# A decode step of attention and a gated MLP: four heads per load of keys or values, 17 loads for 28, with a new order on DVE and PE

## The chip, the cores and the metric

The kernel runs on one core of a Trainium2 chip. The metric is the device time of one execution in microseconds (us), the median of several runs. Engines: PE (matrix multiply), DVE (vector), ACT (scalar functions), POOL (general purpose) and SP, whose queue here does nothing but issue DMAs.

## The reference, cut to what matters

One token x (1 x 576, bf16) is normalized, then goes through attention over the last 4096 positions of a cache with 16 key/value heads, each shared by two query heads (32 query heads of width 128), and through a gated MLP. Both results are added to x.

```
W = 4096                                    # of 65536 positions
q = (xn @ wq).reshape(1, 1, 32, 128)        # wq: 576 x 4096
k = repeat(k_cache[:, :, -W:, :], 2)        # 16 heads x 4096 x 128
v = repeat(v_cache[:, :, -W:, :], 2)
p = softmax(q . k * 128 ** -0.5)
o = (p . v).reshape(4096) @ wo              # wo: 4096 x 576
z = gelu(xn @ w_in)                         # w_in: 576 x 4608
z1, z2 = z[:2304], layernorm(z[2304:])
out = x + o + (z1 * (w_sp * z2 + b_sp)) @ w_out   # w_out: 2304 x 576
```

Keys and values are 16.8 MB each, all inputs that are read 51 MB. Every byte is used once.

## The kernel before, in words

The order of the work is written by hand: each engine runs its instructions in the order in which the program issues them (`manual_schedule`), and waits where a tile is not ready or its buffer is not free.

**Loads.** All large loads are issued by SP, one queue, in program order (L99 to L111): wq in three pieces, the keys of heads 0 to 3, w_in in three pieces, then keys and values in turn, two heads (2.1 MB) per load, then w_out and wo in five pieces. They go into a ring of 7 buffers of 20,736 bytes per partition. A load waits until the readers of the load seven places earlier are done, and every later load on SP waits behind it. In a load of keys, partition r x 2 + h holds 64 consecutive positions of head h (16 KB).

**Start.** xn is laid out in a column, split into XT; 36 matmuls give q (L225, `qps`), which is copied (L232), spread over partitions (L240, `qps2`) and written as `Qb` (L249): for each head four small stationary operands (`be`), one for each part of the transposed layout below. 

**Keys.** Heads are handled in groups of four, g = 0 to 3. `t_half(m, hf)` (L262) turns half of a load of two heads with two DVE transposes of 128 x 1024 fp32 words (each word a pair of bf16), in blocks of 32 x 32. `s_half(m, hf)` (L271) then makes the scores on PE: per head four matmuls (`be`) of 512 columns that accumulate in the PSUM tile `S[g % 2]`, each head at its own 32 columns of the PE (`tile_position`).

**Softmax.** `sm_a(g)` (L296) takes the row maximum on DVE, spreads it over the partitions of a head by two small transposes (`spread`, L284; the whole chain takes 2.3 us, 97.91 to 100.20), and lets ACT write exp of the scores into `pz[g % 2]`, two instructions for a group (L305), with the row sums in `lx`. `sm_b(g)` (L309) transposes `pz` on DVE into `pt` (called tr(g) below) and copies `pt` on ACT into `PT` with 16 small copies (L321), so that positions stand on partitions.

**Values.** `sums(g)` (L324) adds up the row sums with a matmul; `recip(g)` (L331) inverts them. `pv(g)` (L338) is 32 matmuls of 512 columns into the PSUM tile `ops`, at four column positions in turn. `norm(g)` (L351) takes the wanted diagonal of `ops` on DVE, `y_mms(g)` (L361) arranges it on PE, `y_copy(g)` (L371) writes the bf16 column `Y`. The small PSUM tiles (`lps`, `yps`, `psz`) share one buffer, so each waits for the reader of the one before it.

**MLP.** `z_mms` (L375) is 162 small matmuls with w_in as the stationary operand; `z_exp`, `z_gelu` and `z_norm` (L385 to L427) are short DVE, ACT, POOL and PE steps that give `hv`.

**Order.** The loop at L429 runs over 16 halves: transposes of the half, its scores, and between them the softmax of the group before and the values of the group before that. The MLP's DVE work stands in group 1. After the loop (L474): norm and y_mms of group 2, `sm_b(3)`, `pv(3)`, two thirds of `out_hv` (w_out, 36 matmuls in all, L470) while DVE does `norm(3)`, then `y_mms(3)`, the last third, and 64 matmuls of wo (L488), all into `acc`. Two copies and a DMA end the kernel.

Of the kernel before, what the change touches and what calls it, by code (L numbers as in the profile page):

```python
# [22 lines left out]
NT = W // 128  # L23
GK = 4
NG = HKV // GK
NP = HKV // 2
TP = 2 * NT
# [6 lines left out]
RING = 7  # L34
NS = 9
SLOT = NF * D
# [3 lines left out]
def kernel(  # L40
# [19 lines left out]
    ring = ctx.enter_context(tc.tile_pool(name="ring", bufs=RING))  # L60
    const = ctx.enter_context(tc.tile_pool(name="const", bufs=1))
    work = ctx.enter_context(tc.tile_pool(name="work", bufs=2))
    ktpool = ctx.enter_context(tc.tile_pool(name="ktpool", bufs=3))
# [11 lines left out]
    def ring_tile(name, rows, width):  # L75
        t = ring.tile([P, SLOT], BF16, name=name, tag="ring")
        return t[:, 0:rows * width].rearrange("p (s c) -> p s c", c=width)

    def load_halves(src, lo, n, name):

        v = ring_tile(f"{name}{lo}", n, src.shape[1] // 2)
        rows = src.rearrange("r (e c) -> (r e) c", e=2).rearrange("(p s) c -> p s c", s=NS)
        nc.sync.dma_start(v, rows[:, lo:lo + n, :])  # L83
        return [(lo + s, v[:, s, :]) for s in range(n)]

    def load_kv(src, m, name):

        t = ring.tile([P, SLOT], BF16, name=f"{name}{m}", tag="ring")
        v = t[:, 0:TP * DH]
        nc.sync.dma_start(v, src[0, 2 * m:2 * m + 2, SK - W:SK, :].rearrange("h (r t) d -> r h (t d)", t=TP))  # L90
        return v.rearrange("p (t d) -> p t d", d=DH)

    def load_n(src, per, lo, n, name):
        v = ring_tile(f"{name}{lo}", n, D)
        nc.sync.dma_start(v, src.rearrange("(p t) n -> p t n", t=per)[:, lo:lo + n, :])
        return [(lo + t, v[:, t, :]) for t in range(n)]

    K, V = {}, {}
    wq_sb = load_halves(A_wq, 0, 2, "wq") + load_halves(A_wq, 2, 4, "wq") + load_halves(A_wq, 6, 3, "wq")  # L99
    for m in range(2):  # L100
        K[m] = load_kv(A_k_cache, m, "k")
    win_sb = sum((load_halves(B_w_in, lo, 3, "win") for lo in (0, 3, 6)), [])
    for m in range(2, NP):
        K[m] = load_kv(A_k_cache, m, "k")
        V[m - 2] = load_kv(A_v_cache, m - 2, "v")
    for m in range(NP - 2, NP):
        V[m] = load_kv(A_v_cache, m, "v")
    wout_sb = load_n(B_w_out, NF, 0, NF, "wout")
    wo_sb = []
    for n in (14, 9, 6, 2, 1):  # L110
        wo_sb += load_n(A_wo, 32, len(wo_sb), n, "wo")  # L111
# [28 lines left out]
    idv = ident[:].rearrange("p (q c hh) -> p q c hh", q=4, hh=4)[:, :, 0:4, :]  # L140
    cm = const.tile([P, 4], FP32, name="cm")
    nc.vector.tensor_reduce(out=cm[:], in_=idv.rearrange("p q c hh -> p c q hh"), op=ALU.add,
                            axis=mybir.AxisListType.XY)
    dmask = const.tile([P, 4, DH], FP32, name="dmask")
    nc.gpsimd.tensor_copy(dmask[:], cm[:].unsqueeze(2).to_broadcast([P, 4, DH]))
    ohm = const.tile([P, 2, 4], FP32, name="ohm")
    for pr in range(2):
        nc.vector.tensor_reduce(out=ohm[:, pr, :], in_=idv[:, 2 * pr:2 * pr + 2].rearrange("p q c hh -> p hh q c"),
                                op=ALU.add, axis=mybir.AxisListType.XY)
# [3 lines left out]
    selv = sel[:].rearrange("p q (r hh e) -> p q r hh e", r=2, hh=4)  # L153
    for dq in range(4):
        nc.gpsimd.tensor_copy(selv[:, dq, :, :, dq], ohm[:])

    ids = ident[:].rearrange("p (i a h) -> p i a h", i=4, h=2)[:, :, 0:4, :]
    oha = const.tile([P, 4, 2], FP32, name="oha")
    nc.vector.reduce_sum(oha[:], ids.rearrange("p i a h -> p i h a"), axis=AXX)

    lsum = const.tile([P, 4, 8, 2, 2], FP32, name="lsum")
    nc.gpsimd.memset(lsum[:], 0.0)
    for hd in range(2):
        for pr in range(2):
            for th in range(2):
                nc.gpsimd.tensor_copy(lsum[:, 2 * pr + th, 0:4, hd, :],
                                      oha[:, 2 * hd + pr, :].unsqueeze(1).to_broadcast([P, 4, 2]))

    pz = []
    for n in range(2):  # L170
        t = const.tile([P, TP, 16, 2], BF16, name=f"pz{n}")
        nc.gpsimd.memset(t[:], 0.0)
        pz.append(t)
# [88 lines left out]
    def t_half(m, hf):  # L262

        kT = ktpool.tile([P, NT, 2, 16, 2, 2], BF16, name=f"kT{m}_{hf}", tag="kT")
        src = K[m][:, NT * hf:NT * (hf + 1), :].rearrange("p t d -> p (t d)").bitcast(FP32)
        dst = kT[:].rearrange("p t b r x e -> p (t b r x e)").bitcast(FP32)
        for n in range(2):
            nc.vector.transpose(dst[:, 1024 * n:1024 * (n + 1)], src[:, 1024 * n:1024 * (n + 1)])  # L268
        KT[m, hf] = kT

    def s_half(m, hf):  # L271
        g, pr = divmod(m, 2)
        kv = KT.pop((m, hf))[:].rearrange("p t b r x e -> p b e x t r")
        for hd in range(2):
            i = 2 * hd + pr
            for be in range(4):
                nc.tensor.matmul(  # L277
                    S[g % 2][32 * i:32 * i + 8, hf, :],
                    lhsT=Qb[:, 2 * m + hd, be].rearrange("p a h -> p (a h)"),
                    rhs=kv[:, be // 2, be % 2, hd],  # L280
                    start=(be == 0), stop=(be == 3), tile_position=(0, 32 * i),
                )
# [13 lines left out]
    def sm_a(g):  # L296
        s = S[g % 2]
        nc.vector.tensor_reduce(out=mx[:, 0:1], in_=s[:], op=ALU.max, axis=mybir.AxisListType.XY)  # L298
        bk = spread(mx, mb, g, ALU.max, "m")
        nm = work.tile([P, 1], FP32, name=f"nm{g}", tag="nm")  # L300
        nc.vector.tensor_scalar_mul(nm[:], bk[:, 0:1], -SCALE)  # L301
        p = pz[g % 2]
        for hd in range(2):
            lo, hi = 64 * hd, 64 * hd + 64
            nc.scalar.activation(p[lo:hi, :, :, hd], s[lo:hi].rearrange("p a (t r) -> p (a t) r", r=16), ACT.Exp,  # L305
                                 bias=nm[lo:hi, 0:1], scale=SCALE, accum_out=lx[lo:hi, g:g + 1])
        st[g] = {"p": p}

    def sm_b(g):  # L309
        d = st[g]  # L310
        pt = work.tile([P, TP, 32], BF16, name=f"pt{g}", tag="pt")
        src = d["p"][:].rearrange("p t r x -> p (t r x)")
        dst = pt[:].rearrange("p t x -> p (t x)")
        for n in range(2):
            nc.vector.transpose(dst[:, 1024 * n:1024 * (n + 1)], src[:, 1024 * n:1024 * (n + 1)])  # L315
        PT = work.tile([P, 2, TP, 2, 2], BF16, name=f"PT{g}", tag="PT")
        pt4 = pt[:].rearrange("p t x -> p (t x)").bitcast(FP32).rearrange("p (t x) -> p t x", x=16)
        PT4 = PT[:].rearrange("p r t x h -> p (r t x h)").bitcast(FP32).rearrange("p (r t x) -> p r x t", r=2, x=2)
        for i in range(GK):
            for a in range(4):  # L320
                nc.scalar.copy(PT4[32 * a:32 * a + 32, i % 2, i // 2, :], pt4[32 * i:32 * i + 32, :, a])  # L321
        d["PT"] = PT

    def sums(g):  # L324

        lps = ps_m.tile([P, 32], FP32, name=f"lps{g}", tag="m")
        nc.tensor.matmul(lps[:, 0:1], lhsT=lsum[:].rearrange("p q c x h -> p (q c x h)"), rhs=lx[:, g:g + 1],  # L327
# [10 lines left out]
    def pv(g):  # L338

        d = st[g]  # L340
        for tb in range(NT // 4):
            for q in range(4):
                pr, t0 = q // 2, NT * (q % 2) + 4 * tb
                nc.tensor.matmul(  # L344
                    ops[32 * q:32 * q + 16, :],
                    lhsT=d["PT"][:, pr, t0:t0 + 4].rearrange("p t x h -> p (t x h)"),
                    rhs=V[2 * g + pr][:, t0:t0 + 4, :],
                    start=(tb == 0), stop=(tb == NT // 4 - 1), tile_position=(0, 32 * q),
# [79 lines left out]

    for j in range(2 * NP):  # L429
        g, o = divmod(j, GK)  # L430
        t_half(j // 2, j % 2)
        if o == 3:
            if g > 0:
                recip(g - 1)
            if g > 1:
                norm(g - 2)
        s_half(j // 2, j % 2)
        if g > 0 and o == 1:
            if g > 1:
                sm_b(g - 1)  # L440
            else:
                G, sz = z_gelu(*z_exp(zps))

                acc = []
                for n, pool in enumerate((ps_a, ps_b)):
                    t = pool.tile([P, 512], FP32, name=f"acc{n}", tag="ab"[n])
                    acc.append(t[32 * n:32 * n + 1, 0:CW])
                    nc.tensor.matmul(acc[n], lhsT=ones_b[:, 0:1], rhs=xrow[:, CW * n:CW * (n + 1)],
                                     start=True, stop=False, tile_position=(0, 32 * n))
                hv = z_norm(G, sz)  # L450
        if g > 0 and o == 2:
            sums(g - 1)
        if o == 3:
            if g > 1:
                y_mms(g - 2)
            sm_a(g)
            if g > 1:
# [67 lines left out]
```

## Time and profile before

| | us |
|---|---|
| median of 3 runs | 127.36 (127.31 to 127.39) |
| span of the profiled execution | 125.4 |
| between that span and the median of the runs | 1.9 |
| PE, DVE, ACT busy | 68.4, 78.5, 33.6 |
| 32 transposes of keys (L268) | 36.9 |
| 128 score matmuls (L277), union of their records | 32.3 |
| 128 value matmuls (L344), the same | 11.7 |
| 64 copies of PT (L321) | 18.9 |
| 8 exp (L305) | 11.2 |

The span runs from the first to the last instruction of one execution; an execution's own time beside its span is not recorded, so the 1.9 us are taken from the runs. In the rows of the profile, "out<-in" names the tiles written and read, "L" the line above, and what stands behind "<-" in brackets is what ended the idle time before the instruction. The page cuts the span into 40 slices of 3.1 us and gives a digit for the busy share of each, in tenths; DMA is the share of the core's 16 DMA engines, PEclk the clock that PE was granted.

### The profile page before, as it was taken

The page shows a single profiled execution, that of the slowest core. Times are in us where ns is not written, and L with a number is a line of the kernel's source. Part 1 is how long each engine was busy: PE and PEld are TensorE (multiplying, and loading weights), DVE is VectorE, ACT ScalarE, POOL GpSimd, SP SyncE. Part 2 cuts the span into 40 slices and gives each one's busy share as a digit, 9 for nine tenths or more (in the row PEclk, how much of TensorE's full clock was granted, in tenths as well). Part 3 has the DMA queues.
Part 4 walks back from the last instruction along what each step waited for, and adds up shares of the span by engine and source line. Part 5 has one row for each costly group of instructions (what it writes and reads, how often), then busy time and mean ns, then how long its engine had stood idle before and what let it go on. Part 6 is the DMA issues. An engine that isn't in the chain of part 4 may idle for free.

```text
span 125.4 us, 1630 instructions
## 1 busy us (share of the span) xinstructions
PE 68.4 (55%) x626; PEld 31.4 (25%) x626; DVE 78.5 (63%) x150; ACT 33.6 (27%) x85; POOL 7.9 (6%) x27
## 2 busy tenths in 40 slices
PE   0034810398999668069257049639029811178862
PEld 0021110112699612014011012411003511024640
DVE  6853049997517595794798298899098967005001
ACT  4000030000072950000441940260860092920001
POOL 2991000000000000100000000000000000000000
PEclk9999995558975555959958977986955996557998
DMA  4999999999999999999999999999999999999960
GB/s 115 455 423 422 425 434 439 422 428 435 428 438 418 434 434 428 423 444 423 428 439 434 413 439 434 428 428 434 428 436 434 428 426 439 434 409 427 416 261 0
DMA packets 4047, 51.06 MB, mean 407 GB/s; under 512 B 454, under 2 KB 584, under 8 KB 840
## 3 DMA queue, kind: packets, MB, share of 16 engines
q1 hardware_dynamic: 4032, 50.96, 95.6%
q8 instruction: 5, 0.08, 0.2%
q14 instruction: 2, 0.02, 0.0%
q10 hardware_dynamic: 8, 0.00, 0.0%
HBM read 50.96 MB, written 0.00 MB: 406 GB/s over the span
## 4 chain that ended last, share of the span: by engine, by line
DMA 71%; PE 11%; DVE 11%; issue 2%; SPq 1%; ACT 1%
DMA k<-in_A_k_cache_dram 44%; DMA wo<-in_A_wo_dram 17%; DMA wq<-in_A_wq_dram 10%; DVE kT L268 6%; PE S L277 5%; PE ops L344 3%; DVE Qb L255 2%; PE qps L227 1%; PE acc L467 1%; DVE q_rep L238 1%; ACT q_rep L236 1%; DVE on L358 1%; PE lps L327 1%; SPq L83 1%; DVE om L354 1%
## 5 line engine op out<-in xcount | busy, mean ns | idle before, releaser
L277 PE MATMUL S<-kT,Qb 128*8 128x512 bf16 x128 | 32.3, 636 | 30.3 <-DVE kT L268 30.3
L268 DVE STREAM_TRANSPOSE kT<-k 128x1024 f32<-128x1024 f32 x32 | 36.9, 1212 | 8.3 <-DMA k<-in_A_k_cache_dram 8.3
L305 ACT ACTIVATE pz<-S,nm 64x1024 bf16<-64x1024 f32 x8 | 11.2, 1406 | 45.0 <-DVE nm L301 30.3
L321 ACT COPY PT<-pt 32x64 f32<-32x64 f32 x64 | 18.9, 295 | 14.6 <-DVE pt L315 13.8
L277 PEld LDWEIGHTS <-Qb 128*8 128x8 bf16 x128 | 6.4, 96 | 49.7 <-issue 46.7
L344 PE MATMUL ops<-v,PT 128*16 128x512 bf16 x128 | 11.7, 441 | 3.5 <-ACT PT L321 3.5
L315 DVE STREAM_TRANSPOSE pt<-pz 128x1024 bf16<-128x1024 bf16 x8 | 9.4, 1212 | 4.1 <-ACT pz L305 4.1
L380 PEld LDWEIGHTS <-win 128*128 128x128 bf16 x162 | 10.1, 165 | 0.9 <-issue 0.9
L380 PE MATMUL zps<-XT,win 128*128 128x2 bf16 x162 | 10.2, 201 | 0.0
L354 DVE SCALAR_TENSOR_TENSOR om<-ops,rs,dmask 128x512 f32<-128x512 f32 x4 | 3.0, 742 | 7.4 <-PE ops L344 7.3
L298 DVE TENSOR_REDUCE mx<-S 128x1 f32<-128x1024 f32 x4 | 4.9, 1220 | 3.7 <-PE S L277 3.7
L344 PEld LDWEIGHTS <-PT 128*16 128x16 bf16 x128 | 5.0, 97 | 7.3 <-ACT PT L321 4.1
L227 PE MATMUL qps<-wq,XT 128*2 128x512 bf16 x36 | 4.2, 621 | 2.3 <-DVE XT L218 1.9
L467 PE MATMUL acc<-wo,Y 128*1 128x288 bf16 x64 | 4.6, 285 | 1.3 <-DMA wo<-in_A_wo_dram 1.3
L236 ACT CAST q_rep<-qps 128x512 bf16<-128x512 f32 x2 | 1.2, 585 | 14.0 <-DVE q_rep L238 14.0
L238 DVE CAST q_rep<-qps 128x512 bf16<-128x512 f32 x2 | 1.4, 692 | 5.1 <-PE qps L227 4.5
L193 PE MATMUL ps_x<-ones_b,xtw 1*128 1x1 bf16 x9 | 0.4, 162 | 7.2 <-DVE xtw L191 7.2
L492 DVE CAST res<-acc 1x288 bf16<-1x288 f32 x1 | 0.4, 446 | 6.1 <-PE acc L467 6.1
L358 DVE TENSOR_REDUCE on<-om 128x128 f32<-128x512 f32 x4 | 4.1, 1034 | 0.1
L327 PE MATMUL lps<-lx,lsum 128*128 128x1 f32 x8 | 2.1, 333 | 3.2 <-DVE Y L372 3.2
L493 ACT CAST res<-acc 1x288 bf16<-1x288 f32 x1 | 0.4, 389 | 12.4 <-PE acc L467 12.4
L467 PEld LDWEIGHTS <-Y 128*1 128x1 bf16 x64 | 2.9, 83 | 3.0 <-issue 1.9
(90 smaller groups left out, 46.8 us busy)
## 6 DMA issues: line engine op xcount, KB each, us to landing
k<-in_A_k_cache_dram SPq DMA_DIRECT2D x8, 2048.0 KB, 27.2
v<-in_A_v_cache_dram SPq DMA_DIRECT2D x8, 2048.0 KB, 27.8
win<-in_B_w_in_dram SPq DMA_DIRECT2D x3, 1728.0 KB, 27.1
wout<-in_B_w_out_dram SPq DMA_DIRECT2D x1, 2592.0 KB, 30.2
wq<-in_A_wq_dram SPq DMA_DIRECT2D x1, 2048.0 KB, 9.3
wo<-in_A_wo_dram SPq DMA_DIRECT2D x1, 2016.0 KB
wq<-in_A_wq_dram SPq DMA_DIRECT2D x1, 1536.0 KB, 12.5
wo<-in_A_wo_dram SPq DMA_DIRECT2D x1, 1296.0 KB
```

Source lines behind the costliest of these rows:

```text
L227: nc.tensor.matmul(qps[32 * g:32 * g + 2, :], lhsT=XT[:, s, :], rhs=wv[:, 512 * g:512 * (g + 1)], start=(s == 0), stop=(s == NS - 1), tile ...
L268: nc.vector.transpose(dst[:, 1024 * n:1024 * (n + 1)], src[:, 1024 * n:1024 * (n + 1)])
L277: nc.tensor.matmul(S[g % 2][32 * i:32 * i + 8, hf, :], lhsT=Qb[:, 2 * m + hd, be].rearrange("p a h -> p (a h)"), rhs=kv[:, be // 2, be % 2 ...
L298: nc.vector.tensor_reduce(out=mx[:, 0:1], in_=s[:], op=ALU.max, axis=mybir.AxisListType.XY)
L305: nc.scalar.activation(p[lo:hi, :, :, hd], s[lo:hi].rearrange("p a (t r) -> p (a t) r", r=16), ACT.Exp, bias=nm[lo:hi, 0:1], scale=SCALE, ...
L315: nc.vector.transpose(dst[:, 1024 * n:1024 * (n + 1)], src[:, 1024 * n:1024 * (n + 1)])
L321: nc.scalar.copy(PT4[32 * a:32 * a + 32, i % 2, i // 2, :], pt4[32 * i:32 * i + 32, :, a])
L344: nc.tensor.matmul(ops[32 * q:32 * q + 16, :], lhsT=d["PT"][:, pr, t0:t0 + 4].rearrange("p t x h -> p (t x h)"), rhs=V[2 * g + pr][:, t0:t ...
L354: nc.vector.scalar_tensor_tensor(out=om[:].rearrange("p c d -> p (c d)"), in0=ops[:], scalar=d["rs"][:, 0:1], in1=dmask[:].rearrange("p c ...
L358: nc.vector.reduce_sum(on[:], om[:].rearrange("p c d -> p d c"), axis=AXX)
L380: nc.tensor.matmul(zps[:, :, t], lhsT=wt[:, t, :], rhs=XT[:, s, :], start=(s == 0 and t == 0), stop=(s == NS - 1 and t == NF - 1), skip_gr ...
L467: nc.tensor.matmul(acc[n], lhsT=lhs[:, col:col + 1], rhs=wv[:, CW * n:CW * (n + 1)], start=False, stop=last, tile_position=(0, 32 * n))
```

## The change

- **Loads.** A load of keys or values has four heads, a whole group (4.2 MB, 32 KB per partition; partition r x 4 + h, 128 positions each). There are four slots of 32 KB per partition, a to d, one small one (f), and a fixed place for each load: wq (8 rows) in a, wq's ninth row and the last two rows of w_in in parts of d, K0 in b, K1 in c, then w_in a, K2 b, V0 c, K3 d, V1 a, V2 b, V3 c, w_out a, wo in pieces of 18 (d), 10 (b), 3 (c) and 1 (f). All keys are ahead of V1. 17 loads stand where 28 stood. They are still issued by SP in this order.
- **Keys and scores.** `keys(g, c)` turns half of a load of four heads with four transposes of the same size; `scores(g, c)` makes 16 matmuls of 512 columns, with the heads in the inner loop, so that the column position changes with each matmul. The columns are now (pair of position blocks, r, s): neighbouring columns are 128 elements apart. The transposed keys have two buffers of twice the size, not three.
- **Softmax.** exp takes four instructions of 32 partitions for a group. `pz` is one tile for all groups, not two; `pt` is one fp32 tile; the transposes of `sm_b` move fp32 words (two of 1024, as before in number), and its 16 copies have 2 x 64 columns, not 64.
- **Values.** The stationary operand of `pv` has 32 columns, not 16, and all four positions read one load.
- **Constants.** `cm`, `dmask`, `ohm`, `sel`, `oha` and `lsum` follow the new layout with as many or fewer small instructions.
- **Order.** A written list takes the place of the loop. `tail(g)` is recip, norm, y_mms and y_copy. pv(1), tail(1), pv(2) and tail(2) stand after the last scores and ahead of sm_b(3); all of `out_hv` stands behind tail(3).

The diff, cut to its core (what it takes out of the loads and of the loop is in the listing above):

```diff
 W = 4096
 F = 4608
 FH = 2304
...
 GK = 4
 NG = HKV // GK
...
+TP = W // 32
+TC = TP // 2
 NR = 98
 NF = FH // 128
 CW = D // 2
 EPS = 1e-5
 SCALE = DH ** -0.5
 GELU_C = 0.7978845608028654
-RING = 7
 NS = 9
...
     lead = ctx.enter_context(tc.tile_pool(name="lead", bufs=1))
-    ring = ctx.enter_context(tc.tile_pool(name="ring", bufs=RING))
+    big = ctx.enter_context(tc.tile_pool(name="big", bufs=1))
     const = ctx.enter_context(tc.tile_pool(name="const", bufs=1))
     work = ctx.enter_context(tc.tile_pool(name="work", bufs=2))
-    ktpool = ctx.enter_context(tc.tile_pool(name="ktpool", bufs=3))
+    ktpool = ctx.enter_context(tc.tile_pool(name="ktpool", bufs=2))
+    single = ctx.enter_context(tc.tile_pool(name="single", bufs=1))
...
+    def rows(slot, src, name, lo, n, at=None):
+        w = src.shape[1]
+        if at is None:
+            t = big.tile([P, n * w], BF16, name=f"{name}{lo}", tag=slot)[:]
+        else:
+            t = slot[:, at:at + n * w]
+        v = t.rearrange("p (s c) -> p s c", c=w)
+        nc.sync.dma_start(v, src.rearrange("(p s) c -> p s c", p=P)[:, lo:lo + n, :])
         return [(lo + s, v[:, s, :]) for s in range(n)]
...
+    def load_kv(slot, src, g, name):
+        t = big.tile([P, TP * DH], BF16, name=f"{name}{g}", tag=slot)
+        nc.sync.dma_start(t[:], src[0, GK * g:GK * g + GK, SK - W:SK, :].rearrange("h (r t) d -> r h (t d)", t=TP))
+        return t[:].rearrange("p (t d) -> p t d", d=DH)
+    wq_h = A_wq.rearrange("r (e c) -> (r e) c", e=2)
+    win_h = B_w_in.rearrange("r (e c) -> (r e) c", e=2)
     K, V = {}, {}
...
+    rest = big.tile([P, TP * DH], BF16, name="rest", tag="d")
+    wq_sb = rows("a", wq_h, "wq", 0, 8) + rows(rest, wq_h, "wq", 8, 1, 0)
+    K[0] = load_kv("b", A_k_cache, 0, "k")
+    K[1] = load_kv("c", A_k_cache, 1, "k")
+    win_sb = rows("a", win_h, "win", 0, 7) + rows(rest, win_h, "win", 7, 2, 2048)
+    K[2] = load_kv("b", A_k_cache, 2, "k")
+    V[0] = load_kv("c", A_v_cache, 0, "v")
+    K[3] = load_kv("d", A_k_cache, 3, "k")
+    V[1] = load_kv("a", A_v_cache, 1, "v")
+    V[2] = load_kv("b", A_v_cache, 2, "v")
+    V[3] = load_kv("c", A_v_cache, 3, "v")
+    wout_sb = rows("a", B_w_out, "wout", 0, NF)
+    wo_sb = (rows("d", A_wo, "wo", 0, 18) + rows("b", A_wo, "wo", 18, 10)
+             + rows("c", A_wo, "wo", 28, 3) + rows("f", A_wo, "wo", 31, 1))
...
-        t = const.tile([P, TP, 16, 2], BF16, name=f"pz{n}")
...
+    pz = single.tile([P, TC, 8, GK, 2], BF16, name="pz")
+    nc.gpsimd.memset(pz[:], 0.0)
...
-        kT = ktpool.tile([P, NT, 2, 16, 2, 2], BF16, name=f"kT{m}_{hf}", tag="kT")
...
+    def keys(g, c):
+        kT = ktpool.tile([P, TC, 2, 8, GK, 2], BF16, name=f"kT{g}_{c}", tag="kT")
+        src = K[g][:, TC * c:TC * (c + 1), :].rearrange("p t d -> p (t d)").bitcast(FP32)
         dst = kT[:].rearrange("p t b r x e -> p (t b r x e)").bitcast(FP32)
...
+        for n in range(4):
             nc.vector.transpose(dst[:, 1024 * n:1024 * (n + 1)], src[:, 1024 * n:1024 * (n + 1)])
...
-        kv = KT.pop((m, hf))[:].rearrange("p t b r x e -> p b e x t r")
-        for hd in range(2):
...
-            for be in range(4):
+        KT[g, c] = kT
+    def scores(g, c):
+        kv = KT.pop((g, c))[:].rearrange("p (t s) b r x e -> p b e x t r s", s=2)
+        for be in range(4):
+            for x in range(GK):
                 nc.tensor.matmul(
...
-                    lhsT=Qb[:, 2 * m + hd, be].rearrange("p a h -> p (a h)"),
-                    rhs=kv[:, be // 2, be % 2, hd],
-                    start=(be == 0), stop=(be == 3), tile_position=(0, 32 * i),
+                    S[g % 2][32 * x:32 * x + 8, c, :],
+                    lhsT=Qb[:, GK * g + x, be].rearrange("p a h -> p (a h)"),
+                    rhs=kv[:, be // 2, be % 2, x],
+                    start=(be == 0), stop=(be == 3), tile_position=(0, 32 * x),
                 )
...
-        for hd in range(2):
...
-            nc.scalar.activation(p[lo:hi, :, :, hd], s[lo:hi].rearrange("p a (t r) -> p (a t) r", r=16), ACT.Exp,
...
+        for x in range(GK):
+            lo, hi = 32 * x, 32 * x + 32
+            nc.scalar.activation(pz[lo:hi, :, :, x, :], s[lo:hi].rearrange("p a (t r e) -> p (a t) r e", r=8, e=2),
+                                 ACT.Exp, bias=nm[lo:hi, 0:1], scale=SCALE, accum_out=lx[lo:hi, g:g + 1])
+        st[g] = {}
     def sm_b(g):
...
-        pt = work.tile([P, TP, 32], BF16, name=f"pt{g}", tag="pt")
...
+        pt = single.tile([P, TC, 32], FP32, name=f"pt{g}", tag="pt")
+        src = pz[:].rearrange("p t r x e -> p (t r x e)").bitcast(FP32)
         dst = pt[:].rearrange("p t x -> p (t x)")
+        PT = work.tile([P, TC, GK, 2, 2], BF16, name=f"PT{g}", tag="PT")
+        PT4 = PT[:].rearrange("p t x h e -> p (t x h e)").bitcast(FP32).rearrange("p (t x h) -> p t x h", x=GK, h=2)
         for n in range(2):
             nc.vector.transpose(dst[:, 1024 * n:1024 * (n + 1)], src[:, 1024 * n:1024 * (n + 1)])
...
+        for x in range(GK):
             for a in range(4):
-                nc.scalar.copy(PT4[32 * a:32 * a + 32, i % 2, i // 2, :], pt4[32 * i:32 * i + 32, :, a])
...
+                nc.scalar.copy(PT4[32 * a:32 * a + 32, :, x, :], pt[32 * x:32 * x + 32, :, 2 * a:2 * a + 2])
+        st[g]["PT"] = PT
...
+        for tb in range(8):
             for q in range(4):
-                pr, t0 = q // 2, NT * (q % 2) + 4 * tb
+                t0 = 32 * q + 4 * tb
                 nc.tensor.matmul(
-                    ops[32 * q:32 * q + 16, :],
-                    lhsT=d["PT"][:, pr, t0:t0 + 4].rearrange("p t x h -> p (t x h)"),
...
+                    ops[32 * q:32 * q + 32, :],
+                    lhsT=d["PT"][:, t0 // 2:t0 // 2 + 2].rearrange("p t x h e -> p (t x h e)"),
+                    rhs=V[g][:, t0:t0 + 4, :],
+                    start=(tb == 0), stop=(tb == 7), tile_position=(0, 32 * q),
                 )
...
-                    nc.tensor.matmul(acc[n], lhsT=ones_b[:, 0:1], rhs=xrow[:, CW * n:CW * (n + 1)],
...
+    def tail(g):
+        recip(g)
+        norm(g)
+        y_mms(g)
+        y_copy(g)
+    keys(0, 0)
+    scores(0, 0)
+    keys(0, 1)
+    scores(0, 1)
+    keys(1, 0)
+    scores(1, 0)
+    sm_a(0)
+    keys(1, 1)
+    scores(1, 1)
+    zps = z_mms()
+    sm_b(0)
+    sm_a(1)
+    keys(2, 0)
+    scores(2, 0)
+    sm_b(1)
+    zg = z_exp(zps)
+    keys(2, 1)
+    scores(2, 1)
+    G, sz = z_gelu(*zg)
+    acc = []
+    for n, pool in enumerate((ps_a, ps_b)):
+        t = pool.tile([P, 512], FP32, name=f"acc{n}", tag="ab"[n])
+        acc.append(t[32 * n:32 * n + 1, 0:CW])
+        nc.tensor.matmul(acc[n], lhsT=ones_b[:, 0:1], rhs=xrow[:, CW * n:CW * (n + 1)],
+                         start=True, stop=False, tile_position=(0, 32 * n))
+    hv = z_norm(G, sz)
+    sm_a(2)
+    sums(0)
+    pv(0)
+    tail(0)
+    keys(3, 0)
+    scores(3, 0)
+    sm_b(2)
+    keys(3, 1)
+    scores(3, 1)
+    sm_a(3)
+    sums(1)
+    pv(1)
+    tail(1)
+    sums(2)
+    pv(2)
+    tail(2)
+    sm_b(3)
+    sums(3)
+    pv(3)
     def out_mms(lhs, col, wv, last):
         for n in range(2):
...
         for t, wv in wout_sb[6 * c:6 * c + 6]:
             out_mms(hv, t, wv, False)
...
+    tail(3)
+    for c in range(3):
+        out_hv(c)
```

## The prediction

> **What bounds the kernel now.** I read the page first, then the chain of waits, then the timeline from 90 us on.
>
> ```profile
> span 125.4 us, 1630 instructions
> PE 68.4 (55%) x626; PEld 31.4 (25%) x626; DVE 78.5 (63%) x150; ACT 33.6 (27%) x85; POOL 7.9 (6%) x27
> DMA  4999999999999999999999999999999999999960
> q1 hardware_dynamic: 4032, 50.96, 95.6%
> ```
>
> From 3 us to 120 us the DMA row never falls below 9 tenths; no engine is over 63%. The kernel waits for its 50.96 MB. In the chain, rows of the form "start, length, DMA" give landing times:
>
> ```profile
> 1.62 12.45 DMA wq<-in_A_wq_dram
> ...
> 26.14 25.87 DMA k<-in_A_k_cache_dram
> ...
> 61.14 29.70 DMA k<-in_A_k_cache_dram
> ...
> 100.24 21.25 DMA wo<-in_A_wo_dram
> 121.49 0.04 issue
> 121.53 1.46 PE acc L467 x18
> 122.99 0.43 DVE res L492
> ```
>
> Start plus length: wq complete (4.72 MB) at 14.07, heads 6 and 7 of the keys (20.51 MB in all) at 52.01, the last keys (37.29 MB) at 90.84, all but two small pieces of wo (50.51 MB) at 121.49. Between the second and third, 16.78 MB took 38.8 us: 432 GB/s. As long as the queue isn't empty, a load lands at 52.0 us plus (MB before its end minus 20.51)/0.432, whatever the loads are cut into.
>
> How near is the compute chain to being late itself? The timeline:
>
> ```profile
> 98.32 1.89 PE L344 MATMUL ops<-v,PT 128*16 128x512 bf16 x29
> ...
> 103.26 2.37 DVE L315 STREAM_TRANSPOSE pt<-pz 128x1024 bf16<-128x1024 bf16 x2 [1.00 <-ACT pz L305]
> ...
> 105.72 4.90 ACT L321 COPY PT<-pt 32x64 f32<-32x64 f32 x16 [2.49 <-DVE pt L315]
> ...
> 110.67 3.59 PE L344 MATMUL ops<-v,PT 128*16 128x512 bf16 x30 [0.64 <-ACT PT L321]
> ...
> 117.05 1.88 PE L467 MATMUL acc<-wo,Y 128*1 128x288 bf16 x28
> ```
>
> The last group's values end at 114.26; norm and y_mms take 2.2 (the first out_hv after them starts at 116.4), 12 matmuls of out_hv 0.8, 64 of wo 64 x 0.067 = 4.3, and from the last matmul (122.95) to the end of the span lie 2.5. With every byte there, the span would be 114.3 + 2.2 + 0.8 + 4.3 + 2.5 = 124.1. So compute stands only 1.3 us behind the DMA. That is all the cover there is. Two of these rows also show the clock: about the same 30 value matmuls take 1.9 us at 98 and 3.6 at 110.7, after idling; the PEclk row has 9 tenths in the one slice and 5 in the other.
>
> **The change, part by part.**
>
> Bytes: the same. Row packets go from 28 x 128 to 17 x 128, 88 fewer per DMA engine. In the trace's packet records 8,192 bytes take 309 ns and 16,384 take 611, so a packet costs 7 ns beside its bytes; with 11 semaphore packets of 9 ns this saves 0.7 us (bounds 0 and 0.8). If bytes alone set the end: 125.4 - 0.7 = 124.7.
>
> The first load of wq (1.05 MB) took 4.8 us from issue to landing for 2.4 us of bytes, so a load has 2.4 us beside its bytes; behind others in the queue this is hidden, since no slice after 3 us shows a gap. [...]
>
> One load now jumps 16 MiB between four heads; before it jumps as far between two, at 432 GB/s, so I cost this at nothing. [...]
>
> Start: wq comes as 8 rows in one piece, so the first matmul starts at about 12.9, not 11.03, and Qb ends near 23.0, not 21.7. The first keys (4 heads, 8.91 MB) land at 23.8. Hidden, with 0.8 to spare.
>
> Slot waits on SP. Each load waits behind the one before it for its slot; due is when the load ahead lands. K2 free 33 / due 47; V0 46 / 57; K3 and V1 (z_mms) 58 / 67; V2 69 / 86; V3 (pv(0)) 77 / 96; wout (pv(1)) 97 / 105; wo 18 rows 98 / 112; wo 10 (pv(2)) 103 / 118; wo 3 (pv(3)) 117 / 121, with wo 1 behind it. By the 2.4 us above, that much lead is needed. All have it; the last by 1.6 only. So the stream holds, and the end is decided by compute.
>
> Costs that differ per group:
> - keys: 8 transposes of 1.155 (four take 4.62 in the timeline), as before.
> - scores: 32 matmuls. Before, a half of 8 takes 2.0, in records that start in pairs 0.45 apart, two column positions at once. Now four positions alternate, as pv and the q matmuls do, whose records start four at a time. Then 16 take 4 x 0.45 + 0.25 = 2.1; if still two at a time, 4.0. I take 2.1, from pv's fours; the columns, now pairs 256 bytes apart, are in no row.
> - exp: 4 of 1.47, not 2: 5.9 on ACT, in reach of tr(1) but behind DVE elsewhere.
> - copies: 16 of twice the columns. A copy of 64 columns takes 0.306; the exp row has about 1.1 ns per element, so 64 more cost 0.04 to 0.07 at most, and 0.306 is the floor. I take 0.345: 5.5 (4.9 to 6.0).
> - sm_b's transposes: same count, 2.37. pv: same 32, 2.0 warm (2.3 with 32 weight columns: a load of 32 takes 112 ns and of 16 takes 97), 3.6 cold.
> - pz is single: exp(g) waits for tr(g-1), behind which the copies and z's exp queue on ACT. exp(1) ends near 61, just as DVE leaves keys(2,0); no cost. Y and lps share one PSUM buffer, so sums(g) waits for the Y copy before it.
>
> The path, from K2's landing (22.61 MB: 52.0 + 4.9 = 56.9):
> - keys(2,0) 4.6, tr(1) 2.4, z_exp 0.9, keys(2,1) 4.6: DVE at 69.4
> - scores(2,1) 2.1, acc and psz 1.0, rest of z_norm 2.3 (its rows at 49.7 to 52.0): 74.8
> - sm_a(2) 2.3, tail(0) 2.95: 80.1. K3 landed at 76.3 and waits on DVE.
> - keys(3,0) 4.6, tr(2) 2.4, keys(3,1) 4.6: 91.7
> - scores(3,1) 2.1, sums(1) 0.6, pv(1) 2.8 (between warm and cold): 97.2
> - tail(1) 2.6 (114.30 to 116.84 in the timeline), sums(2) 0.6, pv(2) 2.3: 102.7
> - tail(2) 2.6, tr(3) 2.4, copies(3) 5.5: 113.2
> - pv(3) 3.6, cold, PE having idled since 106: 116.8
> - norm and y_mms 2.2, then all 36 out_hv matmuls, which nothing covers any more, 2.4 warm to 3.9: 3.1; wo 4.3; end 2.5: 128.9
>
> So tr(3) starts 2.0 later than before (105.3 against 103.3) although the last scores come 4 us earlier: two pv's and two tails now stand in front of it on DVE and PE. With the longer copies pv(3) ends 2.5 later, and the uncovered out_hv adds 2.3. Against the 124.1 of the chain before this is 4.8 more; the 1.3 of cover goes, and 3.5 shows: 125.4 + 3.5 = 128.9. The median of the runs, 127.36, is 1.9 over the span; 128.9 + 1.9 = **130.8 us**. A measurement here tells about 0.2% (0.25 us) from no change.
>
> **Rivals.**
> - The chain fits under the DMA. It would need 4.2 us off my sum: pv(1) warm 0.8, out_hv warm 0.7, copies at the floor 0.6, K2 earlier by its packets 0.3, and more that I don't see. Then bytes set the end: 124.7 + 1.9 = 126.6, faster by 0.6%. This is the other side; it decides from pv(3) ending before 112.5. For it: the queue is never empty, and K3 is there early. Chance 0.14. Another 0.06 for a chain that just touches the DMA end: 127.1 to 127.6, no change.
> - Scores gain nothing from alternating (two at a time, or the new stride reads at half pace): scores(2,1) and scores(3,1) cost 1.9 more each on the path: 134.6. For it: strided columns are in no fast row, since score matmuls take 0.63 even where the clock is granted (1.00 at 56.7 to 58.8) and pv takes 0.38 there. Chance 0.18.
> - Each of the 11 loads that go saves its 2.4 us beside the bytes: 26 us, 101; the DMA row speaks against it, since the stream hides them. Chance 0.01.
> - The big loads run slower, or the queue runs dry. The lowest full slice in the GB/s row is 409; held throughout, K2 lands 22.61/0.409 - 22.61/0.432 = 2.9 later, and so does everything behind it: 133.7. A slot that comes late past the due times above costs the same way. Chance 0.03.
> - Forecast, with its own range 128.4 to 133.0 (both warm ends off, or both cold): 0.58.
>
> **Range.** From the byte-bound 126.6 to 135.5 (scores at 4.0 and pv(1) cold, 0.8). It leaves out about 1 in 10. Faster by over 0.2% is the first rival and the saved fixed cost: 0.15. Within: 0.06. Slower: 0.18 + 0.03 + 0.58 = 0.79.
>
> **What would show it.** The DMA row stays at 9 up to about 118 us, and the chain of waits no longer ends in DMA wo, but in ACT PT, PE ops and a block of 100 matmuls of acc. A group of 16 scores takes 2.1, with records starting four at a time. The last tr on DVE starts near 105, pv(3) ends near 117, out_hv starts near 119. The step I trust least is scores; the one with most weight is the order on DVE and PE after 91 us. If the last pv ends before 112.5, or the DMA row shows gaps, I am wrong.

## The result and the profile after

| | before | after |
|---|---|---|
| median of the runs, us | 127.41 (127.31 to 127.59) | 132.66 (130.89 to 135.12) |
| profiled execution: span, time, us | 125.4, 127.36 | 131.0, 132.75 |
| last byte of the stream, us | 122.62 | no longer on the path |
| last group's `pv` ends, us | 114.26 | 118.3 |

The ratio is 1.037 (95%: 1.033 to 1.042): the kernel became 3.7% slower. It leaves out two of the six runs after, 134.13 and 135.12, which lie more than 1.5% over the fastest; the median of the other four is 132.56. The forecast was 130.8, with 0.79 on slower. The runs of the changed kernel spread over some 4 us, those of before over 0.3. Steps on PE now stand on the path, and PE's granted clock differs from execution to execution (its mean is 0.768 to 0.815 in the six runs; the 32 matmuls of `pv(2)` take 1.91 in the profiled execution here, mean clock 0.778, and 3.61 in that of e2 below, 0.698). That this makes the spread is likely but not shown, since only one execution of the changed kernel has a trace.

The page of the changed kernel:

```profile
span 131.0 us, 1618 instructions
PE 69.3 (53%) x626; PEld 27.9 (21%) x626; DVE 78.5 (60%) x150; ACT 43.2 (33%) x101; POOL 7.0 (5%) x19
DMA  5979989998998998998999999899999899998100
q1 hardware_dynamic: 2448, 50.96, 91.3%
```

DVE has the 78.5 us that it had, and PE only 0.9 more, yet the span grew by 5.6. ACT has 9.6 more, 7.9 of them in exp (19.1 against 11.2), but in this order the last exp ends at 104.5, well before the transposes that read it start at 107.16. So what changed is mainly the order of the waits. The DMA row, which held 9 tenths nearly to the end, now falls off three slices (10 us) before it; the stream is done, and no engine waits for it. The digits 7 and 8 earlier in the row are no gaps: in stretches of 20 us from 13 to 113 us the DMA engines are busy for 0.98 to 1.02 of the time, at 422 to 440 GB/s. The chain of waits (start, length, engine, tile) has no DMA from 100 us on:

```profile
104.61 0.76 DVE om L335
...
107.16 2.38 DVE pt L299 x2
...
114.70 3.60 PE ops L325 x32
118.33 0.76 DVE om L335
119.12 1.03 DVE on L339
120.19 0.34 PE yps L346 x5
120.63 7.72 PE acc L465 x98
128.35 0.43 DVE res L479
```

Where before 18 matmuls of `acc` followed the last landing, now 100 (the 98 of this row and two ahead of it) follow the last group's tail: all of `out_hv` and of wo. The timeline shows the stretch in which the most was lost against the forecast, the scores:

```profile
56.88 4.62 DVE L254 STREAM_TRANSPOSE kT<-k 128x1024 f32<-128x1024 f32 x4 [5.16 <-DMA k<-in_A_k_cache_dram]
...
69.11 4.02 PE L261 MATMUL S<-kT,Qb 128*8 128x512 bf16 x16 [3.45 <-DVE kT L254]
...
92.85 4.09 PE L261 MATMUL S<-kT,Qb 128*8 128x512 bf16 x16 [2.74 <-DVE kT L254]
...
97.39 2.00 PE L325 MATMUL ops<-v,PT 128*32 128x512 bf16 x32
```

The keys of group 2 land at 56.88 as forecast (56.9). Then each group of 16 scores takes 4.0 to 4.1, not 2.1. In the same row form, 32 matmuls of `pv` with the same number of columns take 2.0.

### The profile page after: what moved, and what is told of

It is laid out like the page before. It is cut to its first block, busy times and chain, and to the rows that moved or that the text cites. A ratio compares the mean times of both kernels' runs of the same rounds, so it can differ in the third digit from the quotient of the medians.

```text
span 131.0 us, 1618 instructions
## 1 busy us (share of the span) xinstructions
PE 69.3 (53%) x626; PEld 27.9 (21%) x626; DVE 78.5 (60%) x150; ACT 43.2 (33%) x101; POOL 7.0 (5%) x19
## 3 DMA queue, kind: packets, MB, share of 16 engines
q1 hardware_dynamic: 2448, 50.96, 91.3%
## 4 chain that ended last, share of the span: by engine, by line
issue 51%; DVE 26%; PE 16%; ACT 4%; POOLq 0%; POOL 0%; DVEq 0%; ACTq 0%
DVE kT L254 7%; PE acc L465 6%; PE ops L325 4%; ACT PT L302 4%; DVE pt L299 4%; PE S L261 3%; DVE on L339 3%; DVE om L335 2%; DVE mx L282 2%; PE yps L346 1%; DVE S L163 1%; DVE xtw L177 1%; POOLq L507 0%; PE ps_x L190 0%; DVE Y L353 0%
## 5 line engine op out<-in xcount | busy, mean ns | idle before, releaser
L288 ACT ACTIVATE pz<-S,nm 32x1024 bf16<-32x1024 f32 x16 | 19.1, 1196 | 37.2 <-DVE nm L285 21.6
L302 ACT COPY PT<-pt 32x128 f32<-32x128 f32 x64 | 19.8, 309 | 17.9 <-DVE pt L299 17.2
L261 PEld LDWEIGHTS <-Qb 128*8 128x8 bf16 x128 | 3.8, 97 | 49.4 <-issue 39.5
L325 PE MATMUL ops<-v,PT 128*32 128x512 bf16 x128 | 9.4, 445 | 7.1 <-ACT PT L302 7.1
L299 DVE STREAM_TRANSPOSE pt<-pz 128x1024 f32<-128x1024 f32 x8 | 9.4, 1211 | 0.8 <-ACT pz L288 0.8
L361 PEld LDWEIGHTS <-win 128*128 128x128 bf16 x126 | 7.9, 164 | 1.9 <-issue 1.9
L361 PE MATMUL zps<-XT,win 128*128 128x2 bf16 x126 | 8.0, 202 | 0.0
L346 PE MATMUL yps<-on,sel 128*32 128x32 f32 x32 | 2.0, 210 | 10.2 <-DVE on L339 10.2
L325 PEld LDWEIGHTS <-PT 128*32 128x32 bf16 x128 | 3.4, 107 | 10.9 <-ACT PT L302 7.2
L346 PEld LDWEIGHTS yps<-on,sel 128*32 128x32 f32 x32 | 1.5, 122 | 12.5 <-DVE on L339 12.5
```

Of the source, the lines that this page charges most:

```text
L261: nc.tensor.matmul(S[g % 2][32 * x:32 * x + 8, c, :], lhsT=Qb[:, GK * g + x, be].rearrange("p a h -> p (a h)"), rhs=kv[:, be // 2, be % 2, x],
L288: nc.scalar.activation(pz[lo:hi, :, :, x, :], s[lo:hi].rearrange("p a (t r e) -> p (a t) r e", r=8, e=2), ACT.Exp, bias=nm[lo:hi, 0:1], sc ...
L302: nc.scalar.copy(PT4[32 * a:32 * a + 32, :, x, :], pt[32 * x:32 * x + 32, :, 2 * a:2 * a + 2])
L325: nc.tensor.matmul(ops[32 * q:32 * q + 32, :], lhsT=d["PT"][:, t0 // 2:t0 // 2 + 2].rearrange("p t x h e -> p (t x h e)"), rhs=V[g][:, t0: ...
L346: nc.tensor.matmul(yps[32 * g:32 * g + 32, :], lhsT=sel[:, dq, :], rhs=d["on"][:, 32 * dq:32 * dq + 32], start=(dq == 0), stop=(dq == 3), ...
L361: nc.tensor.matmul(zps[:, :, t], lhsT=wt[:, t, :], rhs=XT[:, s, :], start=(s == 0 and t == 0), stop=(s == NS - 1 and t == NF - 1), skip_gr ...
```

## The experiments

Theory: the end is set by compute, and three things put it late: the order on DVE and PE after 91 us, `out_hv` without cover behind the last tail, and keys that land in larger loads, so that the first half waits for the second. The scores take 4 us because of where their columns lie. Rivals: the stream itself is slower or lands later with loads of 4 MB; or PE starts only two column positions at a time; or the low granted clock makes the scores slow. Gains in time below are differences between the ratio of the changed kernel (1.037) and that of the run, times 127.4 us; what stands behind +- is an estimate from the two 95% intervals.

**e1_order: the last group's weights ahead of the values of group 2.**

```diff
     pv(1)
     tail(1)
+    sm_b(3)
     sums(2)
     pv(2)
     tail(2)
-    sm_b(3)
     sums(3)
     pv(3)
```

> The changed kernel with one step moved: sm_b(3) stands ahead of sums(2), pv(2) and tail(2), not behind them. Theory (the order on DVE ahead of the last transposes sets the end): tr(3) then waits only for exp(3), which ends at 104.5 in the changed kernel's trace, and starts there and not at 107.2; pv(3) ends near 115.7 and not 118.3; 2.6 us off the span of 131.0, so 128.4. Rival (loads or slots set the end, or the copies on ACT are late for another reason): no change beyond 0.5 us, 131.

Measured: 129.83, ratio 1.019 (1.017 to 1.021), profiled span 128.5: as expected. The timeline:

```profile
104.55 2.37 DVE L299 STREAM_TRANSPOSE pt<-pz 128x1024 f32<-128x1024 f32 x2 [2.35 <-ACT pz L288]
...
107.01 5.04 ACT L302 COPY PT<-pt 32x128 f32<-32x128 f32 x16 [2.49 <-DVE pt L299]
...
112.10 3.60 PE L325 MATMUL ops<-v,PT 128*32 128x512 bf16 x32 [1.27 <-ACT PT L302]
```

The transposes start 2.6 earlier than in the changed kernel (107.16), now released by exp on ACT and no longer by a tail on DVE, and `pv(3)` follows with the same gaps. Here the longer exp does count: four instructions end at 104.5, and the transposes wait 2.35 for them. The order costs 2.3 us (+-0.6), by the profiled spans 2.5.

**e2_cover: `out_hv` beside the last tail.**

```diff
-    tail(3)
-    for c in range(3):
-        out_hv(c)
+    recip(3)
+    out_hv(0)
+    out_hv(1)
+    norm(3)
+    y_mms(3)
+    y_copy(3)
+    out_hv(2)
```

> The changed kernel with the end of the kernel before: two thirds of out_hv stand between pv(3) and norm(3)'s y_mms again, not behind them. Theory (uncovered out_hv is on the path): 24 of the 36 matmuls fall into the 1.9 us in which DVE does norm(3), 2.4 us off the span, so 128.6. Rival (PE's low clock at this point is what costs, and the matmuls take so long that they delay y_mms): under 1 us off, 130 or more.

Measured: 130.32, ratio 1.020 (1.014 to 1.027): about as expected by the time. The profiled execution was the longest of the four (132.05, span 130.2), and its span alone would fit the rival. But it lost its time earlier: `pv(2)` took 3.61 where it takes 1.91 in the trace of the changed kernel. Its timeline:

```profile
102.77 3.61 PE L325 MATMUL ops<-v,PT 128*32 128x512 bf16 x32
...
116.71 3.60 PE L325 MATMUL ops<-v,PT 128*32 128x512 bf16 x32 [6.87 <-ACT PT L302]
...
120.10 2.37 PE L465 MATMUL acc<-wout,hv 128*1 128x288 bf16 x18
...
122.57 1.02 PE L465 MATMUL acc<-wout,hv 128*1 128x288 bf16 x14
123.43 4.08 PE L465 MATMUL acc<-wo,Y 128*1 128x288 bf16 x64
```

Between the end of `pv(3)` and wo, 22 matmuls of `out_hv` now lie beside `norm` and `y_mms`, which take their 2 us anyway; the last 14 (1.0) are all that stays between `y_mms` and wo. From the end of `pv(3)` to the end of the span it takes 130.2 - 120.3 = 9.9 us, against 131.0 - 118.3 = 12.7 in the changed kernel. The missing cover costs 2.2 us (+-1.0) by the ratios, 2.8 in these traces.

**e5_half_loads: each load of keys in two DMAs, four heads by half the positions.**

```diff
-        nc.sync.dma_start(t[:], src[0, GK * g:GK * g + GK, SK - W:SK, :].rearrange("h (r t) d -> r h (t d)", t=TP))
+        rows_in = src[0, GK * g:GK * g + GK, SK - W:SK, :].rearrange("h (r t) d -> r h (t d)", t=TP)
+        for c in range(2 if name == "k" else 1):
+            w = TP * DH // (2 if name == "k" else 1)
+            nc.sync.dma_start(t[:, w * c:w * (c + 1)], rows_in[:, :, w * c:w * (c + 1)])
```

> The changed kernel with the four loads of keys each cut into two DMAs, one for each half that keys(g, c) turns: 21 loads. Theory (the chain that sets the end starts when all of K2 has landed, so the size of a load is on the path): keys(2,0) starts at 52.0 and not 56.9; then exp(1), which ends at 58.8, holds tr(1), so the chain is 2.4 us earlier from keys(2,1) on, and the span 2.4 shorter, 128.6. Rival (K2's landing only happens to precede the chain, and the work of DVE and PE after 70 us is what counts): the gain is lost in later waits, 130.5 or more.

Measured: 128.81, ratio 1.011 (1.006 to 1.016), span 127.3. It gained 3.7 of span where 2.4 were expected:

```profile
52.35 4.62 DVE L257 STREAM_TRANSPOSE kT<-k 128x1024 f32<-128x1024 f32 x4 [2.18 <-DMA k<-in_A_k_cache_dram]
...
57.44 2.37 DVE L302 STREAM_TRANSPOSE pt<-pz 128x1024 f32<-128x1024 f32 x2 [0.47 <-ACT pz L291]
...
111.28 3.60 PE L328 MATMUL ops<-v,PT 128*32 128x512 bf16 x32 [6.87 <-ACT PT L305]
```

The transposes of keys(2,0) start 4.5 earlier than the 56.88 of the changed kernel. I had expected `exp(1)` to hold `tr(1)` back to 58.8; but the first halves of groups 0 and 1 came earlier too, and `tr(1)` started at 57.44. The gain in time is 3.3 us (+-0.8), the largest of e1, e2 and e5, though the intervals overlap. It is not a slower stream: the bytes pass as before (the transposes that wait for the first 20.51 MB start at 52.35; in the kernel before as many bytes had landed at 52.01), only the consumer may start sooner.

**e6_three_parts: e1, e2 and e5 together.**

> The changed kernel with all three repairs: sm_b(3) ahead of pv(2), out_hv around norm(3) as in the kernel before, and each load of keys in two halves. Theory (a compute chain of these three parts sets the end, and the bytes stand behind it): their sum, 2.6 + 2.4 + 3.7, would bring 131.0 to 122.3, which is below what the bytes allow; so the end goes back to the landing of the last rows of wo, and the span is 124.7 to 125.4, a ratio of 0.995 to 1.000 to the kernel before. Rival (the three overlap, or wo's last rows, which wait for pv(3), become late): 126.5 or more.

Measured: 127.67, ratio 1.0017 (1.0007 to 1.0028), span 125.8, 0.4 over the expected range. The end goes back to the DMA. Its timeline:

```profile
107.82 3.60 PE L328 MATMUL ops<-v,PT 128*32 128x512 bf16 x32 [1.26 <-ACT PT L305]
...
117.86 2.37 PE L468 MATMUL acc<-wo,Y 128*1 128x288 bf16 x36 [3.06 <-DMA wo<-in_A_wo_dram]
...
121.30 1.88 PE L468 MATMUL acc<-wo,Y 128*1 128x288 bf16 x28 [1.07 <-DMA wo<-in_A_wo_dram]
```

`pv(3)` ends at 111.4, under the 112.5 from which the bytes should decide; PE then waits twice for wo. The last row of wo lands at 122.66, in the kernel before at 122.62: with 21 loads or 28, with four heads to a load or two, the stream ends at the same time. The small loss fits the 28 matmuls that wait for the last large piece (18 of them before): they end at 123.18, and the 18 ended at 122.95. The three costs alone add up to 2.3 + 2.2 + 3.3 = 7.8 us, and together they give 4.5, which is enough to meet the stream; the rest is hidden. So these three account for the loss.

**e4_flat_columns and e7_flat_whole: the scores read 512 neighbouring columns.** In e4 the matmuls take the blocks in the order in which DVE writes them, and so could also start before the last transpose; in e7 they begin with the last block.

```diff
-                    rhs=kv[:, be // 2, be % 2, x],
+                    rhs=kf[:, 512 * (GK * be + x):512 * (GK * be + x + 1)],            # e4
+                    rhs=kf[:, 512 * (15 - GK * be - x):512 * (16 - GK * be - x)],      # e7
```

> The changed kernel, but each score matmul reads 512 neighbouring columns of the transposed keys in place of its own, which lie 16 bytes apart; this changes which products are added up, so the scores are others, with the same number of matmuls, columns and bytes. Theory (the step between columns makes the read of the keys the limit, about 2.1 columns per ns for all column positions together): four matmuls then take 0.43 or less in place of 0.96, 16 take 2.0 in place of 4.0, and of the 2 x 2.1 us on the path 2.7 to 4.2 show, 127 to 128.5. Rival (the four column positions don't really run at once, or PE's clock limits): 16 still take 4.0 and the span stays at 131.

> As in the kernel that reads 512 neighbouring columns for each score matmul, so with other scores, but in the opposite order over the columns: the first matmuls of a half read what its last transpose writes, so none can start before all four transposes are done, as in the changed kernel. In the first such kernel scores also began during the transposes, so two things were changed in it. Theory (the step between columns alone makes the scores slow): 16 take 1.9 to 2.1, against 4.0; on the path 2 x 2.1 less, and 2.3 more for pv(1) and pv(2) on a PE that has idled, about 129. Rival (the gain came only from starting during the transposes): 16 take 4.0, 131.

Measured: e4 128.55, ratio 1.010 (1.007 to 1.013), span 126.6; e7 131.11, ratio 1.028 (1.027 to 1.030), span 129.4. e4 first:

```profile
86.39 0.60 PE L261 MATMUL S<-kT,Qb 128*8 128x512 bf16 x4 [2.78 <-DVE kT L254]
87.52 0.60 PE L261 MATMUL S<-kT,Qb 128*8 128x512 bf16 x4 [0.53 <-DVE kT L254]
```

The span falls by 4.4, a little more than the 2.7 to 4.2 expected. Four start after each transpose, so its gain has two causes. e7 leaves only the columns. Its clock row and the group:

```profile
PEclk9999995555555555555555555555586555555699
```
```profile
90.98 1.88 PE L261 MATMUL S<-kT,Qb 128*8 128x512 bf16 x16 [4.88 <-DVE kT L254]
```

16 take 1.88, at 5 tenths of the clock. So neither the clock nor the start of the matmuls made 4.1, but the columns. The gain in time is only 1.1 us, 1.6 in the span, about as expected: the blocks are shorter, the pauses before them reach 4.9 us, the clock row stays at 5 tenths up to 94 us, and `pv(1)` and `pv(2)` take 2.65 and 3.60 there (2.00 and 1.91 after).

**e8_step_order: columns without pairing (16 bytes apart, not 256), the pairing done in exp's read.** **e9_heads_outside: the four matmuls of a head one after the other.**

```diff
-        kv = KT.pop((g, c))[:].rearrange("p (t s) b r x e -> p b e x t r s", s=2)
+        kv = KT.pop((g, c))[:].rearrange("p t b r x e -> p b e x t r")                 # e8
...
-        for be in range(4):
-            for x in range(GK):
+        for x in range(GK):                                                            # e9
+            for be in range(4):
```

> The changed kernel with the columns of the scores in the plain order (position block, r), and the pairing done where exp reads the scores. Each matmul then steps 16 bytes from column to column and no longer 256 bytes back and forth. Theory (any stepped read of the keys runs at about 2.1 columns per ns in all): 16 matmuls still take 4.0. Rival (the far step is what costs): they take 2.0, as from four positions at once, and the span falls by up to 4.

> The changed kernel with the loops of the scores exchanged: the four matmuls of a head come one after another, at one column position, as in the kernel before. Theory (the read of the stepped columns is the limit, however many positions run at once): 16 matmuls still take about 4.0 to 4.2, span 131. Rival (the change of position with each matmul is what lets them run together): 4 in a row at one position take 4 x 0.43, 16 take up to 7, and the span rises by up to 6.

One execution each: e8 130.85 (span 129.0), e9 132.44 (span 130.7). Their groups, e8's first:

```profile
92.76 3.85 PE L261 MATMUL S<-kT,Qb 128*8 128x512 bf16 x16 [2.92 <-DVE kT L254]
```
```profile
92.72 4.13 PE L261 MATMUL S<-kT,Qb 128*8 128x512 bf16 x16 [2.62 <-DVE kT L254]
```

Neither moves the 4 us. In both, the matmuls still start in fours. So the rival "two positions at a time" falls (e7's 16, which start in fours too, take 1.88), and so does the step of 256 bytes as the special cause: each of the steps tried does it. The order in which the loops are written does not matter either. Which column positions stand in a four of e9 the trace does not tell.

**e10_filler: 20 matmuls on other data into a free tile, just ahead of `pv(3)`.**

> The changed kernel with 20 more matmuls of 512 columns between sums(3) and pv(3), where PE idles from 107.6 to 114.7; they read values that have landed and write a PSUM bank that is free, and nothing uses the result. Theory (PE comes to pv(3) with the low clock because it has idled, and this is on the path): the fillers take 20 x 0.3 = 6, then pv(3) takes 1.9 and not 3.6, and the 100 last matmuls 6.6 and not 8.0; 3.1 off, a span of 127.9. Rival (the clock is not what makes pv(3) and the last matmuls slow, or the fillers end too late): 131 or more.

Measured: 130.54, ratio 1.021 (1.018 to 1.025), span 129.0, where 127.9 was expected:

```profile
102.64 3.32 PE L325 MATMUL ops<-v,PT 128*32 128x512 bf16 x32
...
108.96 6.17 PE L462 MATMUL S<-v,Qb 128*8 128x512 bf16 x20
116.11 1.91 PE L325 MATMUL ops<-v,PT 128*32 128x512 bf16 x32 [0.98 <-ACT PT L302]
```

Kept busy, PE runs `pv(3)` in 1.91, not 3.60, as meant (the granted clock from 114.5 to 117 is 1.00 here, and 0.53 over `pv(3)` in the changed kernel, 114.70 to 118.30). But in this run `pv(2)` was slow (3.32, not 1.91), and `pv(3)` started 1.4 later, which is more than the 1.1 missed. The last 100 matmuls take 6.3, near the 6.6 expected. The gain in time is 2.0.

**e11_small_pieces: e6 with wo's ten rows in two pieces, 7 and 3. e12_kept_busy: e11 with 16 fillers ahead of wo.**

> The kernel with all three repairs, and the ten rows of wo that land next to last in two pieces of 7 and 3. Theory (the end is now the landing of the last rows, 122.66, and the matmuls that wait for them): 28 matmuls no longer wait together at 121.3; the last ends 0.3 earlier, so 125.5, and the ratio to the kernel before is 0.998 to 1.001; a version clearly faster than the kernel before is not to be had this way, since the last bytes land when they landed there (122.62). Rival (a compute chain still sets the end): no change, 125.8.

> The kernel with the three repairs and wo's rows in smaller pieces, and 16 more matmuls of 512 columns behind out_hv, where PE idles from 114.5 to 117.8; nothing uses their result. In that kernel the first 36 matmuls of wo took 4.0 at the low clock, where with one piece of ten rows they had taken 2.4. Theory (the small pieces would have gained their 0.3, but the clock at the end took 1.6 back and made the later pieces wait): with PE busy the 36 take 2.4, the last pieces' matmuls follow their landings (122.3 and 122.7), the last ends at 122.9 and the span is 125.4 to 125.6, ratio 0.997 to 1.000. Rival (the pieces themselves land later or cost more): 126.0 or more.

Measured: e11 127.88, ratio 1.0036 (1.0022 to 1.0050): a miss, above e6. e12 127.54, ratio 1.0006 (0.9997 to 1.0015). e11's row, then e12's:

```profile
117.82 4.00 PE L469 MATMUL acc<-wo,Y 128*1 128x288 bf16 x36 [3.38 <-DMA wo<-in_A_wo_dram]
```
```profile
119.38 2.33 PE L469 MATMUL acc<-wo,Y 128*1 128x288 bf16 x32
```

After 3.4 us of waiting the 36 matmuls took 4.0 in e11 (2.37 in e6, after 3.1; one execution each, so what decides between them stays open), so that the smaller pieces found PE late. With fillers in that wait, 32 of them take 2.33 and e12 equals the kernel before; its ratio is at the upper end of the 0.997 to 1.000 expected, and its profiled span, 126.3, is that of the longest of its twelve runs. No version beats the kernel before: e6, e11 and e12 all end with the last rows of wo.

## Why the prediction was right, and which term was not

The sum named the bound, the path and nearly all of its steps. That it came within 2.1 us of the span is in part luck: one term was 3.9 too low, and others together 1.8 too high. The times on the path, from the trace of the changed kernel:

| step | forecast, us | measured, us |
|---|---|---|
| group 2's keys land | 56.9 | 56.88 |
| keys(2,0), tr(1), z_exp, keys(2,1) done at | 69.4 | 69.1 |
| scores(2,1) | 2.1 | 4.02 |
| tail(0) done at | 80.1 | 81.5 |
| scores(3,1) | 2.1 | 4.09 |
| sums(1), pv(1), tail(1) | 6.0 | 5.3 |
| sums(2), pv(2) | 2.9 | 2.4 |
| tr(3) and its copies | 7.9 | 7.5 |
| pv(3) | 3.6 | 3.6 |
| out_hv and wo | 7.4 | 8.0 |
| span | 128.9 | 131.0 |

- **The bound.** "The stream holds, and the end is decided by compute": held. The chain has no DMA at its end; e6 shows the point from which it has one again. Every due time of a slot was met; the last piece of wo but one was issued at 118.32, when `pv(3)` freed its slot, and PE came to wo at 123.52 and waited for no DMA. The other signs came 1 to 2 us late, as the longer scores would have it: tr(3) starts at 107.2 (105), `pv(3)` ends at 118.3 (117), `out_hv` starts at 120.3 (119).
- **The scores.** This is the term that failed. I took 2.1 from the fours of `pv` and noted that the new columns were "in no row". The rival that "scores gain nothing from alternating" was priced at 134.6 and came true in its mechanism: 1.9 and 2.0 more. Of its two grounds the runs keep one: the stride of the columns (16 take 1.88 in e7), not the start (in fours, and 4.13, in e9).
- **What offset it.** `pv(1)` and `pv(2)` ran on a high clock (0.94 from 97.39 to 99.39, 1.00 from 102.65 to 104.56). From the end of scores(3,1) to the end of tail(1) that gave 0.7 back, not the full 0.9 of `pv(1)`, because `sm_a(3)` and recip on DVE end at 99.58, after `pv(1)` (99.40): a step that the sum had hidden came onto the path. `pv(2)` gave 0.5. The short times stand behind the longer scores here (in e7, with 16 scores in 1.88, the two take 2.65 and 3.60), but not always: `pv(2)` took 3.61 in e2 and 3.32 in e10. The copies cost 0.314 each, not 0.345 (0.4 in all; the 1.1 ns per element that the estimate took from exp is not what the row gives, 1406/1024 = 1.4, and the copies grew by less than either). The stretches with keys took 0.3 less each time, smaller steps 0.4 less in all, and the end 0.8 more: 0.6 for PE's last matmuls (granted clock 0.66 from 120.6 to 123.5, 0.85 from there to 128.3) and 0.2 behind them. So 3.9 - 1.2 - 0.4 - 0.6 - 0.4 + 0.8 = 2.1, which is the miss in the span.
- **The order and the cover.** I had 2.0 for the later tr(3) and 2.3 for the uncovered `out_hv`; e1 and e2 give 2.3 and 2.2 in time. The 1.3 us of room between compute and DMA before was real: with these two and the large loads undone (e6), the last bytes set the end again.
- **The larger loads.** The sum held their cost, since it started from the landing of all four heads, but the text never priced it: 3.3 in time by e5, 3.7 by the span. It is the largest of the three by its middle value, and the text has only the other side of the ledger, "the last scores come 4 us earlier".
- **The stream.** No fixed cost was saved by fewer loads, as said. Nor did the 0.7 for fewer packets show: the packets' own time fell by 0.3 (95.6% of 125.4 to 91.3% of 131.0), and the last byte with 21 loads came at 122.66 against 122.62. Jumps of 16 MiB between four heads cost nothing: group 2's keys landed to 0.02 us where 432 GB/s puts them, and the last byte of e6, which has the same jumps, came when it came before.

Left open: why the granted clock falls differently from run to run, how much of the spread of the times it makes, and what would happen with e7's columns and the true scores; that needs another layout of the transposed keys, which wasn't tried.

## What to carry to other kernels

Before merging loads, ask what waits for the first byte of each, not how many loads there are: under a full queue the number was free (the last byte came at 122.62 with 28 loads, at 122.66 with 21), and a load of twice the size held its consumer up by 4.5 us. When compute has only some 1 us of room against the stream, a step that is moved ahead of the last group's chain shows in the time (2.3 us in e1), and work that covered a tail must not be put behind it (2.2 in e2). Take the duration of a matmul from a row with the same placement of its columns, not only the same shape: 16 of one shape took 4.09 with the columns apart and 1.88 with neighbouring ones (e7).

## What the runs showed of the hardware

- **Columns apart took one pace.** A score matmul of 512 columns costs, from the spacing of starts, (2.02 - 0.65)/3/2 = 0.23 us in the kernel before (columns 8 bytes apart, two positions), (4.02 - 1.15)/3/4 = 0.24 after (256 and 16 bytes, four positions) and (3.85 - 1.07)/3/4 = 0.23 in e8 (16 bytes, four positions). With neighbouring columns it is (1.88 - 0.63)/3/4 = 0.10 in e7 at 5 tenths of the clock, and (1.91 - 0.38)/31 = 0.05 in `pv` at a granted clock of 1.00. The stepped reads come to 2.1 to 2.2 columns per ns for all positions together. Four positions gave no more than two (2.1 and 2.2), and the clock hardly mattered: before, 8 matmuls take 2.01 us at a granted clock of 1.00 (56.7 to 58.8) and 2.06 at 0.50 (23.9 to 26.0). After, the times of one matmul lie close together too. The row of 8 before, then the single times after (minimum, median, maximum in ns):

```profile
95.80 2.02 PE L277 MATMUL S<-kT,Qb 128*8 128x512 bf16 x8
```
```profile
L261 PE MATMUL S<-kT,Qb x128: 1120/1145/1246, 28.7 to 95.8; 128*8 128x512 bf16 x128
```

  Nor was 8 bytes apart faster than 16 bytes apart (0.23 and 0.23). No run tells the distance between the columns from the shape of the pattern: the slow patterns step in two or three nested loops, the fast ones run straight through 512 columns.
- **Behind idle PE time matmuls were often slow, and fillers helped.** The same 32 matmuls of `pv` take 1.91 at a granted clock of 1.00 and 3.60 at 0.53, behind 7.1 us of waiting (both in the changed kernel), the same 36 of wo 2.37 in e6 and 4.00 in e11. Fillers in the wait got `pv(3)` back to 1.91 (e10) and 32 of wo to 2.33 (e12). How much work keeps the clock up no run here shows.
- **In e4 the clock row and the matmuls disagree.** There PEclk has 9 tenths up to 79 us, yet the 32 matmuls of `pv(0)` take what `pv(3)` takes in the changed kernel at a granted clock of 0.53 (3.60):

```profile
PEclk9999999999999999999999999555577785559599
```
```profile
71.87 3.61 PE L325 MATMUL ops<-v,PT 128*32 128x512 bf16 x32
```

  So a clock read from the row needs a known matmul beside it. In e7 the row and the matmuls agree: 5 tenths from 19 to 94 us, and score matmuls of 585 to 634 ns.
